# Seven block products for seven pairs of steps instead of five, with the splits that feed them moved

## Chip, cores and metric

One core of a Trainium2 chip runs the whole computation in one launch. The metric is the device time of one execution, in microseconds, as the median of several executions. One more execution was profiled; stretches and single instructions below are times in that one, counted from its first instruction.

## What is computed

Attention with a local window of 16 and 24 summary keys (2 batches, 8 heads, 768 positions, 64 per head), then a two-layer network with a leaky activation (512 to 2048 to 512), then four experts, summed with weights. All in fp32, and every number is carried as a sum of two parts, a high one and a low one, so that a product of matrices takes three matmuls: high by high, high by low, low by high.

```python
attn_out = _attn_ref(**attn_kwargs)
x = attn_out.transpose(0, 2, 1, 3).reshape(B * S, H * D)      # 1536 x 512
h = x @ w_in                                                  # 512 -> 2048
x = (np.maximum(h, 0) + alpha * np.minimum(h, 0)) @ w_out     # -> 512
p = domain_probs / (domain_probs.sum(-1, keepdims=True) + 1e-09)
for e in range(4):                                            # the experts: 512 -> 1024 -> 512
    h = np.maximum(x @ w1[e], 0.0)
    out += p[:, e:e + 1] * (h @ w2[e])
```

The change is in the experts alone.

## The kernel before

**Steps.** The 4 x 1024 hidden columns of the experts are cut into 16 (`NQ`) groups of 256, and the 1536 tokens into two batches of 768. A step `s` (0 to 31) is one group for one batch: batch 0 in steps 0 to 15, batch 1 in steps 16 to 31. `standard(s, ...)` issues a plain step, `paired(s, ...)` one whose second layer belongs to a pair.

**First layer of a step** (`e_steps`). A 2 x 2 block product in the Winograd form: seven products `p1, p2, p6, p5, p7, p4, p3` of six matmuls with 384 (`TP`) columns each (`product`, L620). `p1`, `p6`, `p7` and `p4` accumulate in one PSUM buffer (`cb`), `p5` and `p3` in another (`cd`), `p2` in a third (`ca`). Between them ScalarE copies the partial sums out (`keep`, L641: `p`, `u`), and VectorE adds. `result` writes the activation's high part (`gh`, L652, ScalarE) and low part (`gl`, L653, VectorE). `p4` and `p3` of a step are issued in the step behind it (`left`). `cb` and `cd` come from a pool of three PSUM buffers.

**Second layer, plain** (`l2b`). Six blocks of 128 tokens a step, each six matmuls of 512 columns (L508); VectorE multiplies by the expert's weight and adds to `acc` (L778). It runs in the step behind its first layer, after `p7`.

**Second layer, of a pair** (`l2_quad`). For steps `UA <= s < UB` two steps are taken together as a 2 x 2 block product with seven products: 7 x 3 blocks of 128 tokens, each six matmuls of 256 columns (L735), each added by VectorE (L742). It needs sums of the activations (`field`, `s_sums`, `s_split`: VectorE, ScalarE, GpSimd) and sums of the weights, T1 to T4. `UA = 18` and `UB = 28`: five pairs. `fill` lists which of these blocks go between the products of a step.

**Weights.** In batch 0 each step's weights are loaded (`ra`, `rb`), summed (`e_sums`, L392 to L395, GpSimd), and split: high part by ScalarE (L384), low part by GpSimd (L385). Both parts are written to HBM (`put`: `da`, `dw`, `dt`), and batch 1 reads them back (`e_fetch`, `b_load`). `e_prep(s + 1)` lists these pieces of work for the next step; `merge` issues them between the blocks of the second layer. For a pair, the odd step's list ends with `t_sums` (L426, VectorE), which overwrites the raw weights `rb` with T1 to T4; the list of the step behind it holds `t_split` for each of the four (high part L430, ScalarE; low part L431, VectorE), written by `dt`. The raw tiles come from a pool of three buffers (`raw`) and, for odd `rb`, from a single buffer, so the loads behind them wait until they are free. The split parts stand in a free place of `xh` and `xl` (`t_place`) until they are written.

**Second batch's inputs.** `x_combine(1)` splits the blocks of batch 1's input (`x_split`: ScalarE L580, VectorE L581) and forms their sums (L599, VectorE), in steps given by `own_at`.

**What sets the order.** In this part the queues of TensorE and ScalarE are in the order in which the code issues (`manual_schedule`). VectorE, GpSimd and SP are ordered by the compiler's planner, by priority and by its own estimate of when an operand is ready. SP issues all DMAs, in one queue.

Of the kernel before, what the change touches and what calls it, by code (L numbers as in the profile page):

```python
# [8 lines left out]
F32 = mybir.dt.float32  # L9
# [3 lines left out]
ALU = mybir.AluOpType  # L13
# [4 lines left out]
P = 128  # L18
# [21 lines left out]
C0 = 256  # L40
CH = 512
NT = B * S // P
UA, UB = NQ + 2, 2 * NQ - 4

# [46 lines left out]
def kernel(  # L93
# [304 lines left out]
    def quad(s):  # L398
        return UA <= s < UB
# [13 lines left out]
        return hi, lo  # L413

    def t_place(i):
        k, c = 2 * (i % 2), S + 2 * P * (1 + i // 2)
        return slice(None), slice(k, k + 2), slice(c, c + 2 * P)

    def t_view(s, i):
# [43 lines left out]
    def e_prep(s):  # L463
        if s >= 2 * NQ:
            return []
        if s >= NQ:
            return [lambda: e_fetch(s)]

        def part(names, src, pool=wpool[0]):
            pair = e_split(pool, 0, src, len(names) * 2 * P)  # L470
            named(s, names, *pair)
            put(da[s, names[0]], pair)

        def second(i):
            ws[s, i] = e_split(wpool[1], 1, pw["b", s][:, i])
            put(dw[s, i], ws[s, i])

        def flat(t):
            return t.rearrange("p a c -> p (a c)")

        steps = [
            lambda: part(("A11", "A12"), flat(pw["a", s][:, 1:3])),
            lambda: e_sums(s),
            lambda: part(("S1", "S2"), flat(pw["s", s][0])),
            lambda: part(("S3", "S4"), flat(pw["s", s][1])),
            lambda: part(("A22",), pw["a", s][:, 3], wa22),
        ]
        if s + 1 < NQ:
            steps.append(lambda: e_load_a(s + 1))
        for i in range(2):  # L490
            steps.append(lambda i=i: second(i))
        if s + 1 < NQ:
            steps.append(lambda: e_load_b(s + 1))
        if s % 2 and quad(s + NQ):
            steps.append(lambda: t_sums(s))
        elif s % 2 == 0 and quad(s - 1 + NQ):
            for i in range(4):
                steps.insert(2 * i + 1, lambda i=i: t_split(s - 1, i))
        return steps


# [76 lines left out]

    def x_split(b, name, kk, hi, lo, src):
        nc.scalar.activation(hi, src, AF.Copy)  # L580
        nc.vector.tensor_tensor(lo, src, hi.bitcast(F32), op=ALU.subtract)  # L581
        for i, k in enumerate(kk):
            xs[b, name, k] = (hi[:, i], lo[:, i]) if len(kk) > 1 else (hi, lo)

# [39 lines left out]
    bs, fs = {}, {}  # L624

    def field(s, name, f):
        if name == "A12":
            j = (s - UA) // 2
            if (j, name) not in fs:
                fs[j, name] = wp.tile([P, 2, TP], F32, tag="raw", name="a12", bufs=3)  # L630
            return fs[j, name][:, f]
        k = 2 * ("A22", "A11", "A21").index(name) + f
        return acc[:, k * TP:(k + 1) * TP]

    def e_steps(s):
        b = s // NQ
# [69 lines left out]
    def l2_quad(a):  # L706
# [18 lines left out]
        def go(k, i):  # L725
            bname, left, part, first, to = plan[k]
            if k == 0:
                u[i] = ps_2.tile([P, 2, 2 * P], F32, tag="l2", name="l2q")
            ps = u[i][:, part]
            (bh, bl), terms = bs[n, bname], []  # L730
            for f in range(2):
                gh, gl = left(f, 0, i), left(f, 1, i)
                terms += [(gh, bh[:, f]), (gh, bl[:, f]), (gl, bh[:, f])]
            for j, (l, r) in enumerate(terms):
                nc.tensor.matmul(  # L735
                    ps, l, r, start=(first and j == 0), stop=(j == len(terms) - 1), skip_group_check=True
                )
            e = a % NQ * NE // NQ
            for half, d in to:
                t = NAC + half * (NAC // 2) + i  # L740
                dst = acc2[:, t, d * 2 * P:(d + 1) * 2 * P]
                nc.vector.scalar_tensor_tensor(dst, ps, prob_sb[:, t, e:e + 1], dst, op0=ALU.mult, op1=ALU.add)  # L742
            if i == NAC // 2 - 1 and a + 2 < UB:
                b_load(n + 1, bname)

# [142 lines left out]
    with tc.manual_schedule(engines={mybir.EngineType.PE, mybir.EngineType.Activation}):  # L888
        left, keep = [], []
        l2 = l2_steps(len(units) - 1)[KD // 2:]  # L890
        own_at = {NQ - 4: own1[:2], NQ - 3: own1[2:4], NQ - 2: own1[4:], NQ - 1: late1, NQ: last1}

        def standard(s, l2, left):
            p1, p2, p6, p5, p7, p4, p3 = e_steps(s)
            if not left:
                left, l2 = l2[:2], l2[2:]
            for f in [p1] + left[:1] + [p2, p6] + left[1:] + [p5, p7]:
                f()
            side = e_prep(s + 1)
            if s in own_at:  # L900
                side = side[:3] + own_at[s] + side[3:]
            keep = l2[-1:] if s == 2 * NQ - 1 else []
            merge(l2[:len(l2) - len(keep)], side)
            return [lambda i=i, s=s: l2b(s, i) for i in range(NAC)], [p4, p3], keep
# [19 lines left out]
        for a in range(UA, UB, 2):  # L924
            q = l2_quad(a)
            if old is None:
                paired(a, "1.26.57...4...3", left + l2)
                for name in ("T1", "T2", "B22", "T3"):
                    b_load(0, name)
                paired(a + 1, "1.2.6.57..4.3", q[:6])  # L930
# [76 lines left out]
```

## Time and profile before

| | us |
|---|---|
| median of 3 runs | 853.57 (852.83 to 854.12) |
| profiled execution | 852.68 |
| its span, first to last instruction | 850.8 |
| TensorE busy in it | 821.4 |
| VectorE, ScalarE, GpSimd busy | 607.0, 397.6, 218.3 |

The first 337 us are attention and the two-layer network; steps 0 to 15 run from 337 to 595, steps 16 to 31 from there to the end. "Busy" of TensorE counts the modelled lengths of matmuls, which overlap; how fast they follow each other is read from their starts. An idle time stands in brackets behind an instruction, with what ended it.

### The profile page before, as it was taken

The numbers are of one execution on the slowest core, as the hardware profiler recorded it, in microseconds if no ns is written. First come the engines' busy times: TensorE is split into PE (matmuls) and PEld (weight loads), VectorE is DVE, ScalarE is ACT, GpSimd is POOL, SyncE is SP. The second block draws the span as 40 slices with busy tenths as digits, with TensorE's granted clock in tenths as the row PEclk, the third lists the DMA queues.
The fourth block names the chain that finished last, engine by engine and source line by source line (L and its number), as shares of the span: only waits on it lengthen the run. The fifth ranks groups of instructions, "written<-read, shape, count | busy, mean of one in ns | idle before, by whom it ended". The sixth has DMA issues, their size and how long they took to land.

```text
span 850.8 us, 14131 instructions
## 1 busy us (share of the span) xinstructions
PE 821.4 (97%) x4892; PEld 743.9 (87%) x4892; DVE 607.0 (71%) x1274; ACT 397.6 (47%) x982; POOL 218.3 (26%) x206
## 2 busy tenths in 40 slices
PE   4799999999999999899999999999999999999998
PEld 3699999888888888788988988888989999999997
DVE  7998767999983447358587688886556677768555
ACT  5999995544432324344445445443323444443120
POOL 0000000000023100376667668763001232133000
PEclk9699999999999999999999999999999999999999
DMA  8999513333322200367988988959866778787502
GB/s 310 292 284 303 145 45 101 104 94 100 100 87 99 75 1 1 127 242 248 341 298 314 336 296 308 349 209 333 284 212 221 237 248 254 244 251 255 185 14 75
DMA packets 103512, 170.58 MB, mean 200 GB/s; under 512 B 10768, under 2 KB 44560, under 8 KB 103440
## 3 DMA queue, kind: packets, MB, share of 16 engines
q1 hardware_dynamic: 102864, 169.39, 60.2%
q8 instruction: 39, 0.64, 0.3%
q10 hardware_dynamic: 576, 0.28, 0.1%
q14 instruction: 33, 0.27, 0.1%
HBM read 109.86 MB, written 59.77 MB: 199 GB/s over the span
## 4 chain that ended last, share of the span: by engine, by line
PE 70%; DVE 10%; DMA 8%; issue 7%; POOL 2%; ACT 2%; SPq 2%; ACTq 0%; POOLq 0%; DVEq 0%
PE l L508 40%; PE cb L620 11%; PE l2q L735 8%; PE cd L620 5%; PE ca L620 3%; DVE acc L778 2%; DMA raw<-in_wa 2%; DVE xl L431 2%; DMA dw<-w1l 2%; DMA ra<-in_wb 1%; DVE acc L599 1%; PE xps L275 1%; PE s L213 1%; PE pt L257 1%; SPq L406 1%
## 5 line engine op out<-in xcount | busy, mean ns | idle before, releaser
L385 POOL TENSOR_TENSOR w0l<-ra,w0h 128x256 fp32r<-128x256 f32 (+1 forms) x32 | 38.1, 1190 | 344.3 <-ACT w0h L384 341.1
L778 DVE SCALAR_TENSOR_TENSOR acc<-l,prob_sb,acc 128x512 f32<-128x512 f32 x119 | 88.2, 746 | 34.1 <-PE l L508 34.1
L508 PE MATMUL l<-xh,w0h 128*128 128x512 f32 (+1 forms) x240 | 84.5, 352 | 0.0
L508 PE MATMUL l<-gh,w1h 128*128 128x512 f32 (+1 forms) x240 | 83.3, 350 | 0.0
L508 PE MATMUL l<-xl,w0h 128*128 128x512 f32 (+1 forms) x240 | 83.2, 346 | 0.0
L508 PE MATMUL l<-xh,w0l 128*128 128x512 f32 (+1 forms) x240 | 83.1, 346 | 0.0
L508 PE MATMUL l<-gh,w1l 128*128 128x512 f32 (+1 forms) x240 | 82.9, 347 | 0.0
L508 PE MATMUL l<-gl,w1h 128*128 128x512 f32 (+1 forms) x240 | 81.1, 347 | 0.0
L508 PE MATMUL l<-w1h,gh 128*128 128x512 f32 x192 | 75.2, 392 | 2.2 <-DVE acc L778 2.2
L508 PE MATMUL l<-w1h,gl 128*128 128x512 f32 x192 | 75.0, 391 | 0.0
L508 PE MATMUL l<-w1l,gh 128*128 128x512 f32 x192 | 75.0, 391 | 0.0
L704 POOL TENSOR_TENSOR xl<-acc,xh 128x384 fp32r<-128x384 f32 x30 | 31.3, 1058 | 160.2 <-ACT xh L703 155.9
L742 DVE SCALAR_TENSOR_TENSOR acc<-l2q,prob_sb,acc 128x256 f32<-128x256 f32 x120 | 54.3, 477 | 21.8 <-PE l2q L735 20.9
L533 DVE SCALAR_TENSOR_TENSOR l<-m,beta,l 128x512 f32<-128x512 f32 (+1 forms) x60 | 38.5, 644 | 23.8 <-ACT m L527 23.7
L641 ACT ACTIVATE u<-cb 128x384 f32<-128x384 f32 x64 | 31.4, 491 | 45.7 <-PE cb L620 45.5
L527 ACT ACTIVATE m<-l 128x512 f32<-128x512 f32 (+1 forms) x60 | 30.6, 512 | 46.5 <-PE l L508 46.2
L641 ACT ACTIVATE p<-cb 128x384 f32<-128x384 f32 x32 | 15.7, 491 | 74.6 <-PE cb L620 74.6
L508 PEld LDWEIGHTS l<-xh,w0h 128*128 128x128 f32 x240 | 45.4, 189 | 5.9
L508 PEld LDWEIGHTS l<-gh,w1h 128*128 128x128 f32 x240 | 45.4, 189 | 5.6
L508 PEld LDWEIGHTS l<-gh,w1l 128*128 128x128 f32 x240 | 45.4, 189 | 5.6
L508 PEld LDWEIGHTS l<-gl,w1h 128*128 128x128 f32 x240 | 45.4, 189 | 5.6
L508 PEld LDWEIGHTS l<-xh,w0l 128*128 128x128 f32 x240 | 45.3, 189 | 5.7
(166 smaller groups left out, 2418.3 us busy)
## 6 DMA issues: line engine op xcount, KB each, us to landing
raw<-in_wa SPq DMA_DIRECT2D x32, 512.0 KB, 4.0
rb<-in_wb SPq DMA_DIRECT2D x16, 512.0 KB, 5.3
ra<-in_wb SPq DMA_DIRECT2D x32, 256.0 KB, 3.7
dw<-w1h SPq DMA_DIRECT2D x32, 256.0 KB, 4.3
dw<-w1l SPq DMA_DIRECT2D x32, 256.0 KB, 4.0
q<-in_qh SPq DMA_DIRECT2D x24, 256.0 KB, 5.2
dt<-xh SPq DMA_DIRECT2D x20, 256.0 KB, 3.3
dt<-xl SPq DMA_DIRECT2D x20, 256.0 KB, 3.3
```

Source lines behind the costliest of these rows:

```text
L213: nc.tensor.matmul(sp[:, u], q[:, u // 2, u % 2], kw[:, :, u // 2, u % 2], start=True, stop=True)
L385: nc.gpsimd.tensor_tensor(lo, src, hi.bitcast(F32), op=ALU.subtract)
L431: nc.vector.tensor_tensor(lo, t, hi.bitcast(F32), op=ALU.subtract)
L508: ins = nc.tensor.matmul(ps, a, c, start=(i == 0), stop=(i == n - 1))
L527: nc.scalar.activation(m, gs[i, c0][0], AF.Relu, scale=-1.0)
L533: nc.vector.scalar_tensor_tensor(ps, m, beta[:, i:i + 1], ps, op0=ALU.mult, op1=ALU.add)
L620: nc.tensor.matmul(ps, l, r, start=(first and i == 0), stop=(i == len(terms) - 1), skip_group_check=True)
L641: nc.scalar.activation(v[name], ps, AF.Copy)
L704: nc.gpsimd.tensor_tensor(xl[:, k, c], src, xh[:, k, c].bitcast(F32), op=ALU.subtract)
L735: nc.tensor.matmul(ps, l, r, start=(first and j == 0), stop=(j == len(terms) - 1), skip_group_check=True)
L742: nc.vector.scalar_tensor_tensor(dst, ps, prob_sb[:, t, e:e + 1], dst, op0=ALU.mult, op1=ALU.add)
L778: nc.vector.scalar_tensor_tensor(acc2[:, t], ps, pe, acc2[:, t], op0=ALU.mult, op1=ALU.add)
```

## The change

Pairs now cover steps 16 to 29: seven pairs, not five. All else makes room for that or moves with it:

- The four `t_split` of an odd step are issued between the products of that step's own first layer, behind `p1`, `p6`, `p5` and `p7`, and not in the list of weights. They use two places of `xh` and `xl` in turn, not four.
- The odd step's second-layer weights of a pair are written out in the half that is read again.
- Step 0 no longer takes two blocks of the layer before between its products; they follow `p7`.
- `own_at`: B11 in step 11, B21 in step 12, B22 and the first sums in step 14, the second sums and T2, T3 in step 15, T4 in step 16. For batch 1 the low parts of B11, B21, B22 and T1 are made by GpSimd.
- The fields of a pair's activations come from pools, not from `acc`; the first pair's first writes to a part of `acc` multiply and do not add.

```diff
@@ -40,7 +40,7 @@
 C0 = 256
 CH = 512
 NT = B * S // P
-UA, UB = NQ + 2, 2 * NQ - 4
+UA, UB = NQ, 2 * NQ - 2
 
 
 
@@ -413,7 +413,7 @@
         return hi, lo
 
     def t_place(i):
-        k, c = 2 * (i % 2), S + 2 * P * (1 + i // 2)
+        k, c = 2 * (i % 2), S + TP
         return slice(None), slice(k, k + 2), slice(c, c + 2 * P)
 
     def t_view(s, i):
@@ -473,7 +473,8 @@
 
         def second(i):
             ws[s, i] = e_split(wpool[1], 1, pw["b", s][:, i])
-            put(dw[s, i], ws[s, i])
+            n = 2 * P if s % 2 and quad(s + NQ) else DM
+            put(dw[s, i][:, :, 0:n], [x[:, 0:n] for x in ws[s, i]])
 
         def flat(t):
             return t.rearrange("p a c -> p (a c)")
@@ -493,9 +494,6 @@
             steps.append(lambda: e_load_b(s + 1))
         if s % 2 and quad(s + NQ):
             steps.append(lambda: t_sums(s))
-        elif s % 2 == 0 and quad(s - 1 + NQ):
-            for i in range(4):
-                steps.insert(2 * i + 1, lambda i=i: t_split(s - 1, i))
         return steps
 
 
@@ -578,7 +576,8 @@
 
     def x_split(b, name, kk, hi, lo, src):
         nc.scalar.activation(hi, src, AF.Copy)
-        nc.vector.tensor_tensor(lo, src, hi.bitcast(F32), op=ALU.subtract)
+        eng = nc.gpsimd if b and name in ("B11", "B21", "B22", "T1") else nc.vector
+        eng.tensor_tensor(lo, src, hi.bitcast(F32), op=ALU.subtract)
         for i, k in enumerate(kk):
             xs[b, name, k] = (hi[:, i], lo[:, i]) if len(kk) > 1 else (hi, lo)
 
@@ -624,13 +623,15 @@
     bs, fs = {}, {}
 
     def field(s, name, f):
-        if name == "A12":
-            j = (s - UA) // 2
+        j = (s - UA) // 2
+        if name in ("A12", "A21"):
             if (j, name) not in fs:
-                fs[j, name] = wp.tile([P, 2, TP], F32, tag="raw", name="a12", bufs=3)
+                fs[j, name] = wp.tile([P, 2, TP], F32, tag="raw", name="fr", bufs=3)
             return fs[j, name][:, f]
-        k = 2 * ("A22", "A11", "A21").index(name) + f
-        return acc[:, k * TP:(k + 1) * TP]
+        if (j, name, f) not in fs:
+            tag = "t" if name == "A22" else "e"
+            fs[j, name, f] = wp.tile([P, TP], F32, tag=tag, name="f" + tag)
+        return fs[j, name, f]
 
     def e_steps(s):
         b = s // NQ
@@ -739,7 +740,11 @@
             for half, d in to:
                 t = NAC + half * (NAC // 2) + i
                 dst = acc2[:, t, d * 2 * P:(d + 1) * 2 * P]
-                nc.vector.scalar_tensor_tensor(dst, ps, prob_sb[:, t, e:e + 1], dst, op0=ALU.mult, op1=ALU.add)
+                pe = prob_sb[:, t, e:e + 1]
+                if a % NQ == 0 and k in (0, 1, 3, 4):
+                    nc.vector.tensor_scalar(dst, ps, pe, None, op0=ALU.mult)
+                else:
+                    nc.vector.scalar_tensor_tensor(dst, ps, pe, dst, op0=ALU.mult, op1=ALU.add)
             if i == NAC // 2 - 1 and a + 2 < UB:
                 b_load(n + 1, bname)
 
@@ -888,13 +893,16 @@
     with tc.manual_schedule(engines={mybir.EngineType.PE, mybir.EngineType.Activation}):
         left, keep = [], []
         l2 = l2_steps(len(units) - 1)[KD // 2:]
-        own_at = {NQ - 4: own1[:2], NQ - 3: own1[2:4], NQ - 2: own1[4:], NQ - 1: late1, NQ: last1}
+        own_at = {
+            NQ - 5: own1[:1], NQ - 4: own1[1:2], NQ - 2: own1[2:4], NQ - 1: own1[4:] + late1,
+        }
 
         def standard(s, l2, left):
             p1, p2, p6, p5, p7, p4, p3 = e_steps(s)
-            if not left:
+            if s > NQ and not left:
                 left, l2 = l2[:2], l2[2:]
-            for f in [p1] + left[:1] + [p2, p6] + left[1:] + [p5, p7]:
+            t = [lambda i=i: t_split(s, i) for i in range(4)] if s % 2 and quad(s + NQ) else []
+            for f in [p1] + t[:1] + left[:1] + [p2, p6] + t[1:2] + left[1:] + [p5] + t[2:3] + [p7] + t[3:]:
                 f()
             side = e_prep(s + 1)
             if s in own_at:
@@ -924,7 +932,7 @@
         for a in range(UA, UB, 2):
             q = l2_quad(a)
             if old is None:
-                paired(a, "1.26.57...4...3", left + l2)
+                paired(a, "1.26.57...4...3", left + l2, [lambda: None] + last1)
                 for name in ("T1", "T2", "B22", "T3"):
                     b_load(0, name)
                 paired(a + 1, "1.2.6.57..4.3", q[:6])
```

## Rows read from the trace of the kernel before

**Rows 1.** The page, part 1: busy us of each engine, share of span, instructions.

```profile
PE 821.4 (97%) x4892; PEld 743.9 (87%) x4892; DVE 607.0 (71%) x1274; ACT 397.6 (47%) x982; POOL 218.3 (26%) x206
```

**Rows 2.** Busy time by stretch: PE, PEld, DVE, ACT, POOL; clock, DMA share, GB/s.

```profile
336.85:371.02 34.17, 31.12 (x146) 27.56 (x144) 13.94 (x23) 12.27 (x25) 14.85 (x15) 0.95 0.46 168
371.02:529.64 158.62, 156.47 (x782) 140.24 (x781) 117.86 (x168) 74.87 (x150) 107.68 (x96) 1.00 0.86 296
529.64:594.82 65.18, 63.12 (x313) 56.08 (x312) 51.26 (x72) 27.19 (x55) 38.36 (x33) 1.00 0.85 298
594.82:625.84 31.02, 31.02 (x158) 28.13 (x156) 17.35 (x28) 7.68 (x16) 0.00 (x0) 1.00 0.75 256
698.06:727.65 29.59, 29.59 (x213) 29.59 (x212) 21.43 (x45) 12.90 (x28) 8.03 (x8) 1.00 0.76 243
```

**Rows 3.** Timeline of TensorE, 639 to 656: start, length, then the instruction.

```profile
639.72 0.39 PE L508 MATMUL l<-wfh,gh 128*128 128x512 f32 x1
...
642.22 0.39 PE L508 MATMUL l<-wfh,gl 128*128 128x512 f32 x1
...
650.86 0.28 PE L735 MATMUL l2q<-bh,gh 128*128 128x256 f32 x1
...
652.16 0.28 PE L735 MATMUL l2q<-bh,gl 128*128 128x256 f32 x1
...
654.04 0.34 PE L620 MATMUL cd<-xh,wfh 128*128 128x384 f32 x1
...
655.95 0.33 PE L620 MATMUL cb<-xh,wfl 128*128 128x384 f32 x1
```

**Rows 4.** TensorE's waits, 336 to 600: us in total, times, longest.

```profile
PE l L508 <- DVE acc L778: 2.2, 4, 0.8
PE cd L620 <- DVE gl L653: 1.8, 2, 1.3
```

**Rows 5.** Timeline at the start of step 1, 352 to 356, all engines.

```profile
352.83 0.44 PE L620 MATMUL cb<-xh,w0h 128*128 128x384 f32 x1 [2.31 <-ACT w0h L384]
352.86 1.28 POOL L385 TENSOR_TENSOR w0l<-ra,w0h 128x512 fp32r<-128x512 f32 x1 [64.66 <-ACT w0h L384]
...
354.19 0.69 PE L620 MATMUL cb<-xh,w0l 128*128 128x384 f32 x1 [0.74 <-POOL w0l L385]
...
355.00 0.52 PE L620 MATMUL cb<-xl,w0h 128*128 128x384 f32 x1
```

**Rows 6.** Busy time by stretch, behind that wait.

```profile
353.00:357.60 4.60, 3.86 (x13) 3.54 (x14) 0.00 (x0) 2.66 (x6) 4.60 (x5) 0.63 0.84 315
```

**Rows 7.** Timeline at the start of step 3, 385 to 388, all engines.

```profile
385.44 2.54 POOL L385 TENSOR_TENSOR w1l<-rb,w1h 128x512 fp32r<-128x512 f32 x2
...
386.52 0.33 PE L620 MATMUL cb<-xh,w0h 128*128 128x384 f32 x1
...
388.02 0.69 DVE L426 TENSOR_TENSOR rb<-rb 128x512 f32<-128x512 f32 x1 [0.54 <-POOL w1l L385]
```

**Rows 8.** Timeline around the start of step 9, 475 to 487, all engines.

```profile
475.20 0.74 POOL L392 TENSOR_TENSOR s<-ra 128x256 f32<-128x256 f32 x1 [6.22 <-DMA ra<-in_wb]
...
481.46 0.33 PE L620 MATMUL cb<-xh,w0h 128*128 128x384 f32 x1
...
483.99 0.74 POOL L392 TENSOR_TENSOR s<-ra 128x256 f32<-128x256 f32 x1
...
486.70 1.21 DVE L426 TENSOR_TENSOR rb<-rb 128x512 f32<-128x512 f32 x1 [0.16 <-POOL w1l L385]
```

**Rows 9.** Groups by line, 371 to 600: count | busy us, mean ns | idle before.

```profile
L431 DVE TENSOR_TENSOR xl<-rb,xh 128x512 fp32r<-128x512 f32 x20 | 27.3, 1385 | 0.0
...
L430 ACT ACTIVATE xh<-rb 128x512 fp32r<-128x512 f32 x20 | 11.8, 616 | 0.0
...
L599 DVE TENSOR_TENSOR acc<-acc 128x384 f32<-128x384 f32 x8 | 10.0, 1277 | 0.0
```

**Rows 10.** DMA issues, 440 to 560: count, KB each, median us to landing.

```profile
dt<-xh SPq DMA_DIRECT2D x12, 256.0 KB, 3.4
```

## The prediction, made before the change was run

> **What bounds the kernel now.** I read the page's busy shares first: TensorE is busy 821.4 us of a span of 850.8 us [rows 1]. So only two things can move the time: fewer or cheaper matmuls, or less of the 29 us in which TensorE stands still. Next I cut the span into stages, from the first product of one step to that of another [rows 2]. Two standard steps with nothing in their way (594.82 to 625.84) take 31.02 us, 15.51 each, TensorE busy throughout. Two steps whose second layer runs as seven products (698.06 to 727.65) take 29.59 us, again without a hole. The ten steps 2 to 11 take 158.62 us where 10 x 15.51 = 155.1 would do, the four steps 12 to 15 take 65.18 us where 62.0 would: holes of 3.5 and 3.2 us. Steps 0 and 1 take 34.17 us. To see what they need, I took the pitch from starts of matmuls [rows 3]: 512 columns (642.22 - 639.72)/11 = 0.227 us, 384 columns (655.95 - 654.04)/11 = 0.174 us, 256 columns (652.16 - 650.86)/11 = 0.118 us. The stage holds 12 products of six matmuls of 384 columns, three blocks of the layer before (twelve matmuls of 512) and six blocks of step 0's second layer (six of 512): 72 x 0.174 + 72 x 0.227 = 12.5 + 16.4 = 28.9 us. So 5.3 us are holes.
>
> Then I asked who ended these holes [rows 4, 5]. At 352.83 TensorE waited 2.31 us for ScalarE's split of step 1's first weights, then 0.74 us for GpSimd's low half. After it the granted clock fell: 0.63 on the mean of 353 to 357.6 [rows 6], most of that at 1.2 GHz instead of 2.4, and a matmul of 384 columns there is 0.52 us long, against 0.33 elsewhere [rows 3, 5]. That is the rest of the 5.3 us. Four waits are for VectorE's additions to the output (L778), two for the low half of an activation (L653), on which the release of a PSUM buffer hangs [rows 4].
>
> **The change, part by part.** *Two more pairs as seven products.* Per pair 72 matmuls of 512 columns become 126 of 256: by the pitches 72 x 0.227 = 16.36 us against 126 x 0.118 = 14.9 us, and by the stages 31.02 - 29.59 = 1.43 us [rows 2, 3]. Two pairs give **-2.9 us**, all of it on TensorE. The Trainium skill's page "TensorE: Matmul & The Clock Gate", section "Back-to-back issue gap", would make it N/2.4 + 2.5 ns per matmul, 1.78 us a pair and -3.6 us for two; the trace's narrower matmuls pay more than that for their number, so I keep 1.43. The added sums, splits and products of those pairs run on engines that had room in a pair of this kind (VectorE busy 21.4, GpSimd 8.0 of 29.59 us [rows 2]); without that cover a pair would lose at most what VectorE then lacks, and there is none.
>
> *Step 0's order.* The two products of the layer before that filled step 0 (`left`) now come behind its seventh product. 2 x 12 x 0.227 = 5.45 us of TensorE work then lies between that product and step 1, while ScalarE and GpSimd split step 1's weights. The two waits are 2.31 and 0.74 us [rows 5]; 5.45 us cover both, and with them goes the drop of the clock. **-5.3 us.** Inside step 0 the sixth and seventh product now have one product, 6 x 0.174 = 1.04 us, as cover for ScalarE's evacuation of a PSUM buffer, before two products and a block; the nearest row is ScalarE's copy of 512 columns in 0.62 us [rows 9], which one product covers. I take nothing for it, and 0.5 us as its bound.
>
> *Weight sums of the second layer: where they are split.* ScalarE's queue is written by hand. Before, the four splits of an odd step stood among the weight splits, behind the seventh product; now they stand between its products, the first right behind the evacuation of p1. Four low halves of 1.385 us on VectorE [rows 9] leave the stretch where L778 waited; the holes of steps 2 to 11, 3.5 us, are theirs. I take **-3.0 us**, bounds 0 and -3.5. These halves move past the second layer's L778 and in front of the activations' low halves on VectorE, and their eight writes of 256 KB past the weights' writes on SP. The pair's raw weights are also freed some 5 us sooner. The loads of `ra` behind them held GpSimd 6.22 us in one step [rows 8] and should land earlier.
>
> The price: the first split waits for the first of the sums (L426), which waits for GpSimd's last weight split (L385). In step 3 the sums start at 388.02, 1.5 us after that step's p1 (386.52) [rows 7]; in step 9 at 486.70, 5.2 us after its p1 (481.46), because two sums of the next step (from 483.99 on, two of 0.74 us) got in ahead of the last split and the loads were late [rows 8]. What is queued behind this wait on ScalarE: the activation of p4 of the step before, then p2's, then the evacuation `u2` of p6. p5 wants a PSUM buffer that p4's activation and VectorE's L653 release, 5.2 us after p1; p7 wants `u2`. With the sums at +1.5 us the first is done at +2.2 [rows 7], its split of 0.62 us [rows 9] at about +2.8, the activation half a microsecond later, L653 near +4.7 behind one sum and one low half: in time. With the sums at +2.8 and contended, L653 ends near +7: p5 is 2 us late. Per odd step I take 0.7 us with bounds 0 and 2.6; steps 3 to 13 are six: **+4.2 us**, 0 to 15.6. In step 1 no load is late, but its weights are split just before. The first product of step 1 would start at 336.85 + 5 x 1.04 + 3 x 2.73 = 350.3, and GpSimd's first split, now at 352.86 [rows 5], 5.45 us earlier at 347.4; five splits of 1.28 us and one of 0.74 [rows 7] end at 354.5. The sums start 4 us after p1: **+2.0 us**, 1 to 4 with the clock.
>
> The third and fourth split use the two places of the first and second, so they wait until those have landed in HBM: 3.4 us from issue [rows 10]. The fourth is then over near +12 to +14.5, and the next step's weights are split behind it; they are wanted at +15.5. I count this within the 0.7 us.
>
> The odd quad step's second-layer weights are written out half as wide: 0.5 MB less per pair, 3.5 MB over seven pairs, against 2 MB more for each of two added pairs. The DMA share of the stage is 0.86 at 296 GB/s [rows 2], 66 MB over the 224 us; the net of 0.5 MB is under 1% of it. I take zero, and up to 2 us if `ra` lands later instead.
>
> *The second batch's inputs.* Four low halves of `x_split` go from VectorE to GpSimd and are spread over steps 11 to 15. The holes of steps 12 to 15 (3.2 us) hold the two waits for L653 [rows 2, 4], with VectorE held by the sums L599 of 1.28 us mean [rows 9]. These sums stay on VectorE, one step later. I take **-1.2 us**, bounds +1 (GpSimd's split of step 12 delays step 13's sums) and -3.2. T4's splits run beside three second-layer blocks of 6 x 0.227 = 1.36 us; nothing, and up to 1 us if p4 comes before them. The fields moved from `acc` to pools, and the first pair's plain multiply for a multiply-add on VectorE: nothing, the same counts of the same shapes.
>
> **The sum** against the profiled execution, 852.68 us: -2.9 - 5.3 - 3.0 + 4.2 + 2.0 - 1.2 = -6.2, so 846.5. The median of the runs, 853.57, lies 0.9 above it: **847.4 us**.
>
> **The rivals.** *Nothing new waits.* The sums are ready before ScalarE comes to them in every odd step, and all holes go: -2.9 - 5.3 - 3.5 - 3.2 = -14.9 on 853.57, **838.7 us**; with a remainder up to 842. For it: GpSimd idles 6.22 us for a load that should now be early [rows 8]. Against: the last two of six splits end at 387.98 in step 3, 1.5 us after p1, though no load held them [rows 7].
>
> *ScalarE held in every odd step (slower).* The next step's sums still get in ahead of the last weight split, as in step 9. Each odd step then loses about 2.6 us at p5: -2.9 - 5.3 - 3.0 - 1.2 + 3 + 6 x 2.6 = +6.2, about **860 us**. It decides from 10.4/6 = 1.7 us per odd step on; between that and 2.6 the time is 854 to 860. For it: L599 in the same place of step 13 cost TensorE a wait of 1.3 us [rows 4, 9], and a sum that is 0.68 us alone takes 1.21 us beside GpSimd [rows 8]. The Trainium skill's "SBUF — State Buffer", section "Who interferes with whom", has VectorE with two SBUF inputs and a reading GpSimd block each other outright; by that four sums beside GpSimd's cost 4 x (0.68 + 0.74) = 5.7 us, as an estimate, and this rival would be nearer its upper end. The trace's 1.21 us lies a little below 1.42.
>
> *The gap at step 1 stays.* If the planner puts the loads or GpSimd's work so that the weights are late again, 5.3 us of gain are lost: **852.7 us**, no change.
>
> **Chances.** Forecast (842 to 851.8) 0.45, nothing new waits 0.20, no change 0.12, slower 0.23. A measurement of this kernel tells 0.2%, 1.7 us, from no change: faster 0.65, same 0.12, slower 0.23. The range leaves out a tenth at each end: 839.5 to 857.
>
> **What would show it.** Right: quad pairs of 29.6 us from the first step of batch 1; no wait on the weight split near 352; no wait of `l` on L778; odd steps within 1 us of 15.5. Wrong: waits of `cd` on L653 or of `cb` on the evacuation in every odd step, with ScalarE idle in front of `xh<-rb` (L430) until a sum of L426; or even steps that open with a wait on a weight split behind DMA of `dt`.

## The result, and the profile after

The changed kernel took 863.86 us (median of four runs, 862.81 to 864.88); the kernel before, run beside it, 853.85 us. The ratio is 1.0119 [1.0101, 1.0136]: 1.2% slower, where a gain of 6 us was forecast. The profiled execution of after took 864.88 us, its span is 863.1 us.

The busy shares come first, then busy time by stretch, with the columns of [rows 2]. The stretches are steps 0 and 1, steps 2 to 11, steps 12 to 15, and one pair in seven products:

```profile
PE 823.0 (95%) x5000; PEld 750.6 (87%) x5000; DVE 612.8 (71%) x1321; ACT 412.4 (48%) x1018; POOL 231.8 (27%) x227
```

```profile
339.02:372.13 33.11, 30.79 (x146) 27.54 (x145) 18.71 (x31) 14.36 (x29) 12.25 (x11) 0.95 0.60 206
372.13:541.52 169.39, 160.76 (x782) 144.35 (x780) 111.51 (x171) 74.25 (x151) 103.25 (x100) 0.97 0.82 278
541.52:609.84 68.32, 63.50 (x314) 55.96 (x312) 48.52 (x72) 28.34 (x58) 42.18 (x38) 1.00 0.83 283
711.74:741.33 29.59, 29.59 (x213) 29.59 (x211) 21.50 (x45) 12.91 (x28) 8.14 (x8) 1.00 0.78 248
```

TensorE's instructions take almost what they took [rows 1]; the span grew by 12.3 us, 2.2 of them ahead of step 0. Against [rows 2], steps 2 to 11 grew by 10.8 us and steps 12 to 15 by 3.1, while steps 0 and 1 shrank by only 1.1. What lies behind step 16 shrank by 2.7 us (255.98 to 253.25), and a pair in seven products takes the same 29.59 us. (The first product of step 0 starts between 335.8 and 340.6 in the profiles below, though nothing before it was edited; so I compare stages, not distances from the start. The stages come from one execution of each kernel: added up, their difference from the kernel before is up to some 3 us off that of the runs.)

Who ended TensorE's waits, 336 to 610: time in total, count, longest. This answers [rows 4].

```profile
PE cd L619 <- DVE gl L654: 14.1, 8, 3.0
PE l L506 <- DVE acc L783: 1.6, 1, 1.6
```

The four waits for additions to the output (L778 before, L783 now) have become one. In their place p5 (`cd`, L619) waits eight times, once each in steps 1, 3, 5, 7, 9, 11, 12 and 13, for the low half of an activation (L654; L653 before): p4's of the step before, which holds `cd`'s PSUM buffer. The longest wait stands in step 5, whose p1 starts at 420.90. In the timelines below, a row is start, length, instruction, and in brackets the idle time ahead of it with what ended it. ScalarE first, then VectorE, GpSimd and TensorE:

```profile
422.16 0.49 ACT L642 ACTIVATE p<-cb 128x384 f32<-128x384 f32 x1 [4.04 <-PE cb L619]
426.41 0.63 ACT L430 ACTIVATE xh<-rb 128x512 fp32r<-128x512 f32 x1 [3.75 <-DVE rb L426]
426.95 0.47 ACT L653 ACTIVATE gh<-cb 128x384 fp32r<-128x384 f32 x1
427.69 0.49 ACT L642 ACTIVATE u<-cb 128x384 f32<-128x384 f32 x1
```

```profile
425.17 1.94 DVE L426 TENSOR_TENSOR rb<-rb 128x512 f32<-128x512 f32 x2 [0.29 <-POOL w1l L385]
427.02 0.56 DVE L690 TENSOR_TENSOR cd<-cd,u 128x384 f32<-128x384 f32 x1
427.49 0.68 DVE L431 TENSOR_TENSOR xl<-rb,xh 128x512 fp32r<-128x512 f32 x1
428.09 0.68 DVE L426 TENSOR_TENSOR rb<-rb 128x512 f32<-128x512 f32 x1
428.69 0.55 DVE L654 SCALAR_TENSOR_TENSOR gl<-cb,gh 128x384 fp32r<-128x384 f32 x1
```

```profile
421.89 1.30 POOL L385 TENSOR_TENSOR w1l<-rb,w1h 128x512 fp32r<-128x512 f32 x1
423.14 0.74 POOL L393 TENSOR_TENSOR s<-s,ra 128x256 f32<-128x256 f32 x1
423.84 1.29 POOL L385 TENSOR_TENSOR w1l<-rb,w1h 128x512 fp32r<-128x512 f32 x1
```

```profile
429.29 0.69 PE L619 MATMUL cd<-xh,w0h 128*128 128x384 f32 x1 [3.00 <-DVE gl L654]
429.78 0.52 PE L619 MATMUL cd<-xl,w0h 128*128 128x384 f32 x1
430.10 0.52 PE L619 MATMUL cd<-xh,w0l 128*128 128x384 f32 x1
```

Read from the bottom up, this is the chain of the slower rival. TensorE waits 3.00 us for `gl`, which stands on VectorE behind a sum and a low half of the weights. `gl` needs `gh` (426.95), which stands on ScalarE behind the first split L430. That split found ScalarE idle for 3.75 us, until the first sum L426. And the sums waited for GpSimd's last weight split, ahead of which a sum of the next step (L393) got in.

After the wait the matmuls of 384 columns start 0.32 us apart (429.78, 430.10), not 0.174. Busy time and granted clock by stretch, ahead of the wait and behind it (the clock is the third number from the right), and then behind the waits of step 3 (1.95 us), step 11 (2.32) and step 13 (2.92):

```profile
424.00:426.20 2.20, 2.20 (x14) 1.97 (x12) 1.60 (x2) 0.00 (x0) 1.83 (x2) 1.00 0.87 245
429.40:434.50 5.10, 5.10 (x15) 4.89 (x16) 3.01 (x6) 1.54 (x4) 0.00 (x0) 0.50 0.81 259
```

```profile
395.00:399.90 4.90, 4.90 (x24) 4.43 (x25) 4.85 (x9) 2.70 (x6) 0.00 (x0) 1.00 0.70 240
...
529.70:533.50 3.80, 3.80 (x15) 3.62 (x16) 2.71 (x6) 1.39 (x3) 0.00 (x0) 0.64 0.80 275
...
566.20:570.00 3.80, 3.80 (x20) 3.50 (x21) 3.20 (x6) 1.81 (x5) 0.00 (x0) 1.00 0.62 208
```

0.50 is 1.2 GHz of 2.4. So step 5 is 21.49 us long: 15.51, 3.0 of waiting and some 2.8 of slow matmuls. Step 3 lost its wait alone (17.76), step 11 again both (19.67). Odd steps of after, with ScalarE's idle time ahead of the first L430, and p5's wait:

| step | 1 | 3 | 5 | 7 | 9 | 11 | 13 |
|---|---|---|---|---|---|---|---|
| length, before | 18.18 | 15.73 | 16.55 | 16.13 | 16.48 | 16.19 | 17.50 |
| length, after | 19.59 | 17.76 | 21.49 | 16.15 | 16.78 | 19.67 | 20.65 |
| ScalarE idle, after | 2.96 | 3.43 | 3.75 | 1.85 | 2.37 | 3.06 | 3.68 |
| p5's wait, after | 2.32 | 1.95 | 3.00 | 0.37 | 0.98 | 2.32 | 2.92 |

### The profile page after: what moved, and what is told of

Its sections match the earlier page's. It is cut to its first block, busy times and chain, and to the rows that moved or that the text cites. A ratio compares the mean times of both kernels' runs of the same rounds, so it can differ in the third digit from the quotient of the medians.

```text
span 863.1 us, 14540 instructions
## 1 busy us (share of the span) xinstructions
PE 823.0 (95%) x5000; PEld 750.6 (87%) x5000; DVE 612.8 (71%) x1321; ACT 412.4 (48%) x1018; POOL 231.8 (27%) x227
## 4 chain that ended last, share of the span: by engine, by line
PE 65%; issue 10%; POOL 8%; DMA 7%; ACT 5%; DVE 4%; SPq 1%; POOLq 0%; DVEq 0%; ACTq 0%
PE l L506 34%; PE l2q L736 12%; PE cb L619 10%; PE cd L619 5%; POOL w0l L385 4%; DMA ra<-in_wb 3%; PE ca L619 2%; POOL w1l L385 2%; ACT sm L232 1%; ACT sm L251 1%; PE s L213 1%; PE xps L275 1%; POOL s L393 1%; DMA raw<-in_wa 1%; DMA q<-in_qh 1%
## 5 line engine op out<-in xcount | busy, mean ns | idle before, releaser
L385 POOL TENSOR_TENSOR w0l<-ra,w0h 128x256 fp32r<-128x256 f32 (+1 forms) x32 | 35.5, 1108 | 377.4 <-ACT w0h L384 377.4
L783 DVE SCALAR_TENSOR_TENSOR acc<-l,prob_sb,acc 128x512 f32<-128x512 f32 x101 | 74.5, 748 | 34.7 <-PE l L506 34.6
L747 DVE SCALAR_TENSOR_TENSOR acc<-l2q,prob_sb,acc 128x256 f32<-128x256 f32 x156 | 70.6, 478 | 29.7 <-PE l2q L736 28.5
L705 POOL TENSOR_TENSOR xl<-ft,xh 128x384 fp32r<-128x384 f32 x14 | 15.9, 1138 | 141.7 <-ACT xh L704 141.7
L506 PEld LDWEIGHTS l<-xl,w0h 128*128 128x128 f32 x240 | 45.4, 189 | 5.5
```

Source lines behind the costliest of these rows:

```text
L385: nc.gpsimd.tensor_tensor(lo, src, hi.bitcast(F32), op=ALU.subtract)
L506: ins = nc.tensor.matmul(ps, a, c, start=(i == 0), stop=(i == n - 1))
L705: nc.gpsimd.tensor_tensor(xl[:, k, c], src, xh[:, k, c].bitcast(F32), op=ALU.subtract)
L747: nc.vector.scalar_tensor_tensor(dst, ps, pe, dst, op0=ALU.mult, op1=ALU.add)
L783: nc.vector.scalar_tensor_tensor(acc2[:, t], ps, pe, acc2[:, t], op0=ALU.mult, op1=ALU.add)
```

## The experiments

Theory: ScalarE, held at the first split, delays p4's activation and so p5. Rivals: VectorE has too much to do, wherever the splits stand; or the second batch's inputs or GpSimd are to blame. Stage lengths in us, from the profile of each kernel; time and ratio from the runs (ratio against the kernel before on the same chip, 95% interval):

| run | 0–1 | 2–11 | 12–15 | from 16 | median | ratio |
|---|---|---|---|---|---|---|
| before | 34.17 | 158.62 | 65.19 | 255.98 | 853.85 | 1 |
| after | 33.11 | 169.39 | 68.32 | 253.25 | 863.86 | 1.0119 [1.0101, 1.0136] |
| e1_splits_behind_p7 | 30.12 | 166.08 | 69.07 | 253.31 | 857.17 | 1.0047 [1.0029, 1.0065] |
| e2_order0_only | 29.03 | 158.95 | 65.92 | 256.00 | 848.50 | 0.9948 [0.9932, 0.9964] |
| e3_second_first | 30.86 | 173.03 | 67.84 | 253.23 | 863.99 | 1.0128 [1.0101, 1.0156] |
| e4_splits_only | 35.43 | 167.74 | 63.93 | 256.07 | 860.72 | 1.0085 [1.0064, 1.0106] |
| e5_splits_as_before | 29.25 | 159.35 | 68.31 | 253.28 | 852.53 | 0.9989 [0.9969, 1.0008] |
| e6_as_before_low_gpsimd | 29.03 | 174.37 | 71.68 | 253.18 | 864.28 | 1.0129 [1.0093, 1.0164] |
| e7_inputs_vector | 33.19 | 170.17 | 66.52 | 253.71 | 862.56 | 1.0113 [1.0082, 1.0143] |
| e8_low_gpsimd | 33.27 | 169.21 | 66.92 | 253.20 | 864.54 | 1.0132 [1.0097, 1.0166] |
| e9_splits_behind_p5 | 29.87 | 159.29 | 69.47 | 253.44 | 850.63 | 0.9975 [0.9956, 0.9993] |
| e10_six_pairs_as_before | 29.25 | 160.17 | 64.30 | 255.22 | 848.77 | 0.9954 [0.9937, 0.9971] |
| e11_six_pairs_behind_p5 | 29.88 | 158.73 | 67.17 | 255.21 | 848.71 | 0.9953 [0.9937, 0.9969] |
| e12_inputs_as_before | 29.25 | 159.80 | 69.19 | 253.74 | 853.18 | 1.0000 [0.9988, 1.0012] |
| e13_behind_p5_inputs_as_before | 29.87 | 158.40 | 71.60 | 253.81 | 853.93 | 0.9999 [0.9982, 1.0016] |
| e14_six_pairs_new_inputs | 29.25 | 159.45 | 67.52 | 254.80 | 849.32 | 0.9955 [0.9940, 0.9970] |

**One part alone: the moved splits.** The kernel before with the splits between the products, and nothing else:

```diff
-        elif s % 2 == 0 and quad(s - 1 + NQ):
-            for i in range(4):
-                steps.insert(2 * i + 1, lambda i=i: t_split(s - 1, i))
...
-            for f in [p1] + left[:1] + [p2, p6] + left[1:] + [p5, p7]:
+            t = [lambda i=i: t_split(s, i) for i in range(4)] if s % 2 and quad(s + NQ) else []
+            for f in [p1] + t[:1] + left[:1] + [p2, p6] + t[1:2] + left[1:] + [p5] + t[2:3] + [p7] + t[3:]:
```

> The kernel before with the splits of the weight sums between the products of their own odd step as in the changed kernel, for its five pairs and with its four places; nothing else changed. Theory A: this part alone makes the loss; steps 3 to 11 take 8 to 12 us more than in the kernel before, 861 to 866 us. Theory B' (the loss comes from the two more pairs, the second batch's splits on GpSimd or the narrower places): 850 to 856 us.

With the old number of pairs, the old inputs and four places for the splits, the move alone makes steps 2 to 11 9.1 us longer; the time, 860.72 us, is at the lower edge of theory A's range. The waits that are new against [rows 4], 336 to 600 (L650 is `gl` there):

```profile
PE cd L617 <- DVE gl L650: 10.3, 5, 2.6
```

**One part alone: step 0's order.**

```diff
-            if not left:
+            if s > NQ and not left:
```

> The kernel before with step 0's order alone: the two blocks of the layer before behind p7. Prediction's step: the wait of 2.3 and 0.7 us at step 1 and the fall of the clock behind it go, 5.3 us: 848 to 850 us. Rival: step 1's weights are late from another cause, so that the hole stays where it was: 853 to 854 us.

```profile
335.79:364.82 29.03, 29.03 (x146) 26.09 (x145) 14.48 (x23) 12.40 (x25) 15.23 (x15) 1.00 0.57 200
```

Steps 0 and 1 take 29.03 us, TensorE busy throughout at full clock: 5.1 us less than in [rows 2], for 28.9 worked out. This one line is worth half a per cent and beats both kernels.

**The splits behind the products.** After, with two splits behind p7 and two in the next step's side work:

```diff
-            for f in [p1] + t[:1] + left[:1] + [p2, p6] + t[1:2] + left[1:] + [p5] + t[2:3] + [p7] + t[3:]:
+            for f in [p1] + left[:1] + [p2, p6] + left[1:] + [p5, p7] + t[:2]:
...
+            if t:
+                side[4:4] = t[2:3]
+                side[6:6] = t[3:]
```

> The changed kernel with the four splits of the weight sums behind p7 of their odd step (two at once, two among the next step's weight splits), all else the same. Theory A: ScalarE's queue is held by the first split until the first sum (L426) is there, and with it the activation of p4 that p5's PSUM buffer waits for. Then the waits of cd for the low half of an activation in steps 1 to 13 go, the odd steps fall from 16.2 to 21.5 us to 15.5 to 16.5, and the time to 843 to 849 us. Theory B: VectorE has too much to do in an odd step, wherever the splits are queued. Then the holes only move behind p7 (waits of l for the additions to acc) and the time stays at 858 us or more.

Up to step 11 p5 doesn't wait. But VectorE now makes two low halves back to back while GpSimd works, and an addition to the output stands behind them. VectorE in step 3, and the waits for that line:

```profile
394.50 3.42 DVE L431 TENSOR_TENSOR xl<-rb,xh 128x512 fp32r<-128x512 f32 x2
397.85 2.06 DVE L783 SCALAR_TENSOR_TENSOR acc<-l,prob_sb,acc 128x512 f32<-128x512 f32 x3
```

```profile
PE l L506 <- DVE acc L783: 7.7, 6, 2.0
```

So p5's hole in these steps comes with the splits' place on ScalarE, as theory A had it, but a bad place for the low halves makes another one, as theory B had it. The time, 857.17 us, lies between the two.

**The first split behind p5.** After, with the four splits spread further back; up to step 10 their writes get four places again (kernel e4 had those too, so they are not what matters):

```diff
-            for f in [p1] + t[:1] + left[:1] + [p2, p6] + t[1:2] + left[1:] + [p5] + t[2:3] + [p7] + t[3:]:
+            for f in [p1] + left[:1] + [p2, p6] + left[1:] + [p5] + t[:1] + [p7] + t[1:2]:
...
+            if t:
+                side[1:1] = t[2:3]
+                side[3:3] = t[3:]
```

> The changed kernel, with the second layer's weight splits later in ScalarE's queue: the first behind p5, the second behind p7, the third and fourth in the next step's side list (places 1 and 3), with four places for their writes up to step 10. Theory (what costs time is that ScalarE stands at the first split, with p4's activation of the step before queued behind it): with the first split behind p5 neither that activation nor the evacuation that p7 wants is held; the waits before p5 fall from the 2 to 3 us of the kernel after to below 0.5 us, the ten steps 2 to 11 take 159 to 163 us (169.4 after; 166.1 with all splits behind p7), and the whole some 846 to 852 us. Rival (VectorE has too much to do beside GpSimd, wherever the splits stand): the waits only move to the additions to the output, as with the splits behind p7; steps 2 to 11 take 166 us or more and the whole 855 us or more.

Steps 2 to 11 take 159.29 us, ten less than after's. In steps 1 to 11 p4's activation comes 2.30 us behind p1 and its low half 2.83. ScalarE and VectorE in step 5 (p1 at 417.43):

```profile
419.73 0.49 ACT L653 ACTIVATE gh<-cb 128x384 fp32r<-128x384 f32 x1
426.08 0.49 ACT L653 ACTIVATE gh<-cd 128x384 fp32r<-128x384 f32 x1 [3.72 <-DVE cd L690]
426.47 0.62 ACT L430 ACTIVATE xh<-rb 128x512 fp32r<-128x512 f32 x1
```

```profile
420.26 0.56 DVE L654 SCALAR_TENSOR_TENSOR gl<-cb,gh 128x384 fp32r<-128x384 f32 x1 [1.88 <-ACT gh L653]
424.37 1.21 DVE L426 TENSOR_TENSOR rb<-rb 128x512 f32<-128x512 f32 x1 [1.85 <-POOL w1l L385]
```

The sums are as late as in after (+6.94 us against +4.27), and the same splits run. Only what stands behind the waiting split has changed (and the places, which e4 had too). This settles the theory for steps 2 to 11, against VectorE's load as such.

**The splits as in the kernel before.** After, with the splits' old loop and old place in the side work, four places but for steps 11 and 13:

```diff
-        k, c = 2 * (i % 2), S + TP
+        k, c = 2 * (i % 2), S + TP if s > NQ - 6 else S + 2 * P * (1 + i // 2)
...
+        elif s % 2 == 0 and quad(s - 1 + NQ):
+            for i in range(4):
+                steps.insert(2 * i + 1, lambda i=i: t_split(s - 1, i))
```

> The changed kernel with the splits of the weight sums where the kernel before had them, between the weight splits of the next step, with four places for steps 1 to 9 and two for 11 and 13; all else of the change stays. Behind p7 in a row left holes of 1.0 to 2.2 us a step before the additions to acc, because two low halves came back to back on VectorE. Theory C: the place in the queues is all of the loss. Then the odd steps lose what they lost before, 0.2 to 1.0 us, and 853.2 - 5.0 (step 0's order) - 2.9 (two pairs) + 1 to 2 (steps 1 and 13 now have sums and splits) gives 845 to 848 us. Rival: the added sums and splits of steps 1 and 13 and the second batch's inputs cost as much as two pairs give: 850 us or more.

Steps 2 to 11 fall to 159.35 us, as in e9: theory C for these steps. Steps 12 to 15 keep 68.3, to which I return, and the time, 852.53 us, is the rival's: no gain over the kernel before that the runs can tell.

**Sums earlier.** After, with the second layer's weight splits of an odd quad step's preparation (`second`) ahead of its sums and first-layer parts, so that GpSimd is done with them sooner:

```diff
+        early = s % 2 and quad(s + NQ)
+        if early:
+            steps[1:1] = [lambda i=i: second(i) for i in range(2)]
...
-        for i in range(2):
-            steps.append(lambda i=i: second(i))
+        if not early:
+            steps += [lambda i=i: second(i) for i in range(2)]
```

> The changed kernel, with the splits of an odd step's second-layer weights ahead of those of its weight sums S1 to S4 and A22 on ScalarE and GpSimd; the splits of T1 to T4 stay between the products. Theory A: GpSimd's last split that the sums wait for ends some 3.3 us earlier (two splits of 1.28 us and one of 0.74 move behind it), the first sum starts before or at p1 instead of 1.5 to 4.3 us after it, and the waits of cd shrink below 0.5 us a step: 843 to 850 us. Theory B (VectorE's load): the waits stay, 858 us or more. A third outcome, that S1 to S4 are now late for p6 and p7, would show waits of cb and cd for w0l.

From step 3 to 11 the first sum comes up to 0.3 us ahead of p1 and ScalarE doesn't idle, but p5 still waits 1.7 to 2.1 us in each odd step, and the time stays (863.99 us). Step 3, p1 at 384.25; VectorE, then TensorE:

```profile
383.94 1.76 DVE L426 TENSOR_TENSOR rb<-rb 128x512 f32<-128x512 f32 x1
385.63 0.74 DVE L786 SCALAR_TENSOR_TENSOR acc<-l,prob_sb,acc 128x512 f32<-128x512 f32 x1
386.29 2.27 DVE L426 TENSOR_TENSOR rb<-rb 128x512 f32<-128x512 f32 x2
388.48 1.22 DVE L431 TENSOR_TENSOR xl<-rb,xh 128x512 fp32r<-128x512 f32 x1
389.62 1.21 DVE L426 TENSOR_TENSOR rb<-rb 128x512 f32<-128x512 f32 x1
390.75 0.54 DVE L657 SCALAR_TENSOR_TENSOR gl<-cb,gh 128x384 fp32r<-128x384 f32 x1
```

```profile
391.35 0.44 PE L622 MATMUL cd<-xh,w0h 128*128 128x384 f32 x1 [1.72 <-DVE gl L657]
```

`gh` was there 2.3 us after p1 (386.55), but VectorE is filled up to 390.83 with four sums that take 1.1 to 1.8 us each beside GpSimd, not 0.68 as alone, and with other work between them. So there are two queues in series ahead of `gl`, and freeing ScalarE's shows VectorE's. My expectation for this run missed that.

**Low halves on GpSimd, inputs on VectorE.** In e8 after's L431 runs on GpSimd; in e7 `x_split` uses VectorE for all pieces; in e6 e5's low halves run on GpSimd:

```diff
-        nc.vector.tensor_tensor(lo, t, hi.bitcast(F32), op=ALU.subtract)
+        nc.gpsimd.tensor_tensor(lo, t, hi.bitcast(F32), op=ALU.subtract)
```

> The changed kernel with the low halves of T1 to T4 on GpSimd, the splits still between the products. If ScalarE's wait for the sums alone delays p5, nothing moves: 861 to 864 us. If VectorE's queue, sums and low halves in front of L654, is the longer part, p5 comes 0.7 to 1.2 us sooner in seven steps: 855 to 859 us.

> The changed kernel with the second batch's low halves back on VectorE. Prediction's step: moving them to GpSimd is worth 1.2 us at most 3.2, so 864 to 867 us. Rival: on GpSimd they stand in front of step 13's weight splits and made part of that step's 5 us: 858 to 862 us.

> The same, and the low halves of T1 to T4 on GpSimd instead of VectorE. If VectorE's queue makes what is left of the odd steps' holes, the waits of l for the additions to acc go and the time falls 2 to 4 us below the run with the low halves on VectorE: 842 to 845 us. Rival: GpSimd, four more splits of 1.3 us in front of the next step's weight splits, is then late for p1 of the even steps (waits of cb for w0l): 848 us or more.

Neither e8 nor e7 moves the time by more than the runs' intervals: ScalarE idles at its first split as it does in after (2.4 to 4.2 us in e8). e7's 862.56 us lies between its two ranges; in step 13 p5 waits 3.18 us with the second batch's low halves on VectorE, for 2.92 in after, so it is not their place on GpSimd that makes that wait. e6 shows what GpSimd's delay does in the old order. Waits of e8, then of e6, same columns as above:

```profile
PE cd L619 <- DVE gl L654: 15.8, 8, 3.7
```

```profile
PE cb L622 <- ACT p L645: 13.8, 7, 3.3
PE cd L622 <- DVE gl L657: 4.9, 2, 3.2
```

In e6 GpSimd comes later to the next step's sums. From 372 to 541 ScalarE's weight splits wait 17.4 us for those sums (L393; 6.2 us in the kernel before) and 14.4 us for the next load of `ra`, and the evacuation `p` of p1 stands on ScalarE behind them: 174.4 us for steps 2 to 11, by a wait that neither expectation named. In that order the low halves belong on VectorE.

**Six pairs.** To find what makes steps 12 to 15 longer: e10 is e5 with six pairs, `own_at` of the kernel before (without its last entry), low halves on VectorE and four places throughout; e11 is the same with e9's order; e12 and e13 are e10 and e11 with seven pairs; e14 is e5 with six pairs and nothing else.

```diff
-UA, UB = NQ, 2 * NQ - 2
+UA, UB = NQ, 2 * NQ - 4
...
-            NQ - 5: own1[:1], NQ - 4: own1[1:2], NQ - 2: own1[2:4], NQ - 1: own1[4:] + late1,
+            NQ - 4: own1[:2], NQ - 3: own1[2:4], NQ - 2: own1[4:], NQ - 1: late1,
```

> The changed kernel with the weight splits placed as in the kernel before, with six pairs of seven products rather than seven, the second batch's early pieces in the same steps as in the kernel before and its low halves on VectorE. What is left of the change is step 0's order, one more pair and the new homes of the fields. Theory: terms of the sum add up: step 0 and 1 take 29.2 us (34.2 before), steps 2 to 11 some 159 us, steps 12 to 15 some 65 to 66 us (68.3 with seven pairs and the splits as before), and the rest 254.6 us (1.4 below before); the whole about 847 us. Rival (the moved fields or the smaller halves of the second pair's buffers cost the steps 12 to 15 their time, not the number of pairs): steps 12 to 15 stay near 68 us and the whole at 850 us or more.

> The kernel with the first split behind p5, with six pairs and the second batch's pieces as in the run with six pairs. Theory (the place of ScalarE's first split sets the odd steps): steps 2 to 11 as in the run with seven pairs and the first split behind p5, within 1 us (159 to 163), steps 12 to 15 some 2 us shorter than there, the whole 846 to 850 us. Rival (VectorE's load): 166 us or more for steps 2 to 11, and the whole 853 us or more.

> Seven pairs of seven products, the weight splits as in the kernel before, and the second batch's input pieces in the steps and on the engine of the kernel before. Against the run with seven pairs and the splits as before, only the pieces' steps and their engine differ; against the run with six pairs, only the number of pairs. Theory (the new steps of the second batch's pieces, two steps running with one piece more behind weight splits, cost steps 12 to 15 their extra 4 us): steps 12 to 15 as with six pairs, 64.3 us within 1.5, the rest behind step 16 as with seven pairs, 253.3 us; by stages 338 + 29.2 + 159.8 + 64.3 + 253.3 = 845, with 1.7 us around the span some 846 us. Rival (it is the seventh pair's, whose buffers or loads reach back into steps 12 to 15): they take 68 us or more, and the whole 850 us or more.

> The same, with the first split behind p5 rather than as in the kernel before: all of the change but the first place of the splits and the pieces of the second batch. Theory: steps 2 to 11 some 159 us, steps 12 to 15 as in the run with six pairs and this order (67.2 us, within 1), behind step 16 253.3 us; the whole 847 to 849 us. Rival (the seventh pair): 69 us or more for steps 12 to 15, and 851 us or more.

> The run with the splits as in the kernel before and seven pairs, now with six pairs and nothing else different: the second batch's pieces stay in the change's steps (11, 12, 14, 15), with their low halves on GpSimd. Theory (the seventh pair's sums and splits, which fall to steps 13 and 14, cost steps 12 to 15 their time): these steps take 64 to 65.5 us as in the other run with six pairs (64.3), and the time is near that one's, 847 to 849 us. Rival (the new steps of the pieces cost it): they stay at 67.5 us or more, and behind step 16 1.5 us are added, so 851 us or more.

In e12 and e13 step 13's splits overwrite some columns of the second batch's pieces, so from there on they compute with other inputs, in the same work, and what they put out is wrong. ScalarE waits for that too (e12):

```profile
563.29 0.63 ACT L430 ACTIVATE xh<-rb 128x512 fp32r<-128x512 f32 x1 [1.57 <-DVE xl L582]
```

They can't settle the question therefore; e14 does in part. With six pairs and the change's inputs, steps 12 to 15 take 67.52 us, near the 68.31 of seven pairs and far from e10's 64.30. So, by one profile each, the pair costs 0.8 us there, and 3.2 us come from what else e14 has over e10: the pieces' steps and engine, and two places for step 11's splits. ScalarE's row and VectorE's behind it, in step 11 to 12, and p5's wait in step 12:

```profile
524.58 0.64 ACT L430 ACTIVATE xh<-rb 128x512 fp32r<-128x512 f32 x1 [2.47 <-DMA dt<-xh]
```

```profile
525.00 2.56 DVE L601 TENSOR_TENSOR acc<-acc 128x384 f32<-128x384 f32 x2
528.14 1.68 DVE L601 TENSOR_TENSOR acc<-acc 128x384 f32<-128x384 f32 x1
529.75 1.76 DVE L431 TENSOR_TENSOR xl<-rb,xh 128x512 fp32r<-128x512 f32 x1
533.16 0.54 DVE L657 SCALAR_TENSOR_TENSOR gl<-cb,gh 128x384 fp32r<-128x384 f32 x1
```

```profile
533.76 0.44 PE L622 MATMUL cd<-xh,w0h 128*128 128x384 f32 x1 [3.16 <-DVE gl L657]
```

A split waits for its place's last write to land, the weight splits start late behind it, and VectorE's sums and low halves run beside GpSimd ahead of `gl`. Which of the two, places or pieces, weighs more stays open.

What the pairs are worth on the whole is read from the ratios. With five pairs and step 0's order (e2) it is 0.9948, with six (e10, e11, e14) 0.9953 to 0.9955, with seven and the splits in a better place (e5, e9) 0.9989 and 0.9975. So no run shows a gain of a sixth pair over e2, and with the seventh, which is all that e5 has over e14, the kernel is some 3 us slower, by intervals that just touch.

## Why the prediction was wrong

By stages the sum had -3.3, +0.5, -0.5 and -2.9 us for steps 0 and 1, 2 to 11, 12 to 15 and what follows; measured were -1.1, +10.8, +3.1 and -2.7.

**The price of the moved splits: the step that failed.** I took 0.7 us per odd step, from a first sum at +1.5 us after p1 (step 3, [rows 7]). The steps were seen right, queue by queue, and so was what decides: the activation of p4 and L653 behind the waiting split. The size was wrong, and I had set it by the row that was best for the change. The first sum came at +2.9 to +4.7 us in steps 3 to 13, not +1.5: the next step's sums still went ahead of GpSimd's last split, as in step 9 [rows 8]. The excess over 15.51 us is 2.25, 5.98, 0.64, 1.27, 4.16 and 5.14 us in steps 3 to 13, 3.2 on the mean, above the 1.7 at which the rival decides and above its 2.6. Of these 19.4 us 11.5 are p5's waits, 1.6 the wait for L783 in step 13, and some 4.8 the rest of steps 5 and 11, where the clock was down behind the wait; I had priced the clock at step 1 and at no other. The last 1.5 us are not traced to a wait. The sums did come sooner in steps 5 to 11, as the earlier loads promised (+5.2 to +2.9 us in step 9). But none came early enough for p5, and step 3's came later. In e4 one step met my condition, step 3 with its p1 at 387.10 (ScalarE, VectorE, TensorE):

```profile
389.32 0.64 ACT L430 ACTIVATE xh<-rb 128x512 fp32r<-128x512 f32 x1 [0.47 <-DVE rb L426]
391.67 0.55 DVE L650 SCALAR_TENSOR_TENSOR gl<-cb,gh 128x384 fp32r<-128x384 f32 x1
392.32 0.39 PE L617 MATMUL cd<-xh,w0h 128*128 128x384 f32 x1
```

The first sum is at +1.5 us, the low half at +4.6, and p5 starts without a wait, as I had it, with 0.1 us to spare. In after, which also has a pair in step 1, the same step's first sum is at +3.95. And e3 shows that an early sum is not enough: at -0.3 us it runs beside GpSimd, and `gl` comes at +6.5 us in step 3, held by VectorE's queue instead.

**The gain of the moved splits: smaller than forecast.** The four waits on L778 (2.2 us, in steps 5, 7, 9 and 11) are gone; the one of 1.6 us on L783 is in step 13. My -3.0 gave these waits nearly all of the stage's 3.5 us, where [rows 4] had 2.2. And the gain was bought: e4 has it and the price alone, and loses 9.1 us in steps 2 to 11.

**Step 0's order: right.** -5.3 forecast, -5.1 in e2's stage. In after it is hidden: p5 of step 1 waits 2.32 us, and with the clock step 1 is 4.1 us too long, where I took 2.0, with a bound of 4.

**Two pairs: right where they run, not on the whole.** -2.9 forecast, -2.7 measured behind step 16. By the formula of the Trainium skill's "TensorE: Matmul & The Clock Gate", "Back-to-back issue gap", -3.6 us was to be had, as an estimate; the section gives that formula for a matmul by itself. This trace's stream keeps nearer to the stages' 1.43 us a pair (1.37 measured). But I priced the pairs where they run, not where their weights are prepared: in the runs the sixth brings no gain, and the seventh a loss (e5 against e14).

**The second batch's inputs: the gain did not come.** Forecast -1.2. In after steps 12, 14 and 15 take 47.67 us, for 47.69 before, and step 13's loss is the price above; so the pieces bring nothing, and with the splits put back (e14 against e10) their new steps and engine and the two places together cost 3.2 us. The runs tell no difference by their engine (e7: 862.56 us, after: 863.86), though steps 12 to 15 are 1.8 us shorter in e7's profile. Whether my bound of +1 holds for the pieces alone stays open. That two places make the split wait for its write was seen, and counted within the 0.7.

**The rivals.** The slower one was right in mechanism and named its sign: waits of `cd` on L653 in odd steps, ScalarE idle ahead of L430. Its 860 us is 3.9 short: by stages 1.7 of that lie in steps 12 to 15, 1.2 in steps 0 and 1, 0.8 in steps 2 to 11. What spoke for it stood in the rows: 1.5 us in step 3 with no load late, and 5.2 in step 9. I let the best of them carry the forecast, and the rival got 0.23.

## What to carry to other kernels

In a queue written by hand, the place of an instruction is priced by what stands behind it times the lateness of what it waits for, and that lateness is taken from the worst rows, not from the best. Follow the released buffer through every queue on its way: clearing ScalarE's only showed VectorE's. Where a change has several parts, the cheap one may be all of its worth: here one condition (e2) gives 0.5%, and no run with more of the change came out faster than that. A part that gains where it runs, like the pairs, can lose as much where it is prepared.

## What the runs showed of the hardware

- A sum of 512 columns on VectorE takes 0.68 us alone (428.09 in after). In e3's steps 5, 7 and 9 the three of each step that run beside GpSimd take 1.56 us on the mean and 1.81 at the longest. The Trainium skill's "SBUF — State Buffer", "Who interferes with whom", says that a VectorE instruction with two SBUF inputs contends with a GpSimd instruction that reads SBUF, and that the ports they share are an exclusive lock. My estimate of 1.42 us took that with GpSimd's sums of 0.74 us; with its splits of 1.30 us the same rule gives up to 1.98, as an estimate, and these sums stay below it.
- The granted clock did not follow the length of a wait: behind 2.32 us in step 11 it was 0.64 and behind 3.00 in step 5 0.50, but behind 2.92 in step 13 1.00; in e3 it was 0.70 behind 1.72 us in step 3 (391.4 to 396). So a wait cost its length, or about twice that, and the length alone did not tell which. (Before, one of 2.31 us brought 0.63 [rows 5, 6].)
